# Local and global attention with a gated feed-forward layer: loads paced in the planner, exponentials of 21 tiles turned by transfers, and every engine's order laid anew

## The chip, the cores and the metric

The kernel runs on one core of a Trainium2 chip. A core has five instruction streams: TensorE (PE, matrix products, with its weight loads shown as PEld), VectorE (DVE), ScalarE (ACT), GpSimd (POOL) and SyncE (SP). SP does no arithmetic here; it issues transfers, as GpSimd does too. The transfers themselves run on 16 DMA engines that all streams share. The metric is device time in microseconds (us), lower is better; a profile is one more execution, whose span is counted from its first to its last instruction.

## What is computed

Eight batches of eight heads attend over 32 global and 512 local positions; a local query sees the global keys and the local keys at most 32 positions away. All 544 output positions of a batch then go through a feed-forward layer. Cut to what matters:

```python
s_g   = scale * q_g @ concat(k_g, k_l).T
out_g = softmax(s_g) @ concat(v_g, v_l)
s_ll  = where(abs(i - j) <= 32, scale * q_l @ k_l.T, -1e9)
out_l = softmax(concat(scale * q_l @ k_g.T, s_ll)) @ concat(v_g, v_l)
x = concat(out_g, out_l).reshape(8 * 544, 512)       # heads side by side
h = x @ w_in                                          # 512 -> 2048
out = (h * clip(h + 3, 0, 6) / 6) @ w_out             # 2048 -> 512
```

## The kernel before

**Units of work.** Local attention works on 32 tiles, one for each batch b and each 128 queries j. A tile passes through: S, the scores of its eight heads (line 810, 32 short matmuls); per head a mask-and-maximum on DVE (822) and an exponential on ACT (826); E, the turning of the exponentials; A, their product with the values (853); a normalisation on DVE (865, 867); X, the turning of the result into `xt`. E and X are done either on PE with a copy out of PSUM (839 and 874, copies at 372 on ACT and 374 on DVE), or by a transposing transfer that SP issues (354); the strings `ETURN` and `XTURN` say which for each tile. Each batch also has one global tile (Sg line 912, Ag line 956). Queries and keys of a batch are turned on PE in one of two forms, 64 small matmuls (691) or 32 larger ones (728); `WIDE` lists the batches of the second form. The values are loaded to `vn`, and A needs them in overlapping strips `vs`; a strip is either copied ("moved", 634 on ACT, 636 on DVE and POOL) or transferred by SP (608 and the transfer below it); `MOVED` and `MOVERS` say which, and by which engines.

**Feed-forward.** M1 (994) makes one of 16 column chunks of the hidden layer with four matmuls, ACT and DVE gate it (1000, 1004), M2 (1020) multiplies by `w_out`, ACT or DVE copies the result out (1031, 1033), SP stores it. Batch 0 does M1 in halves of 256 tokens, the others with 512.

**Loads.** Nearly all loads from memory convert to fp16 and are issued by GpSimd (344). GpSimd also moves strips, in one order with the loads.

**Order.** No order is written by hand. The program first runs a planner (`Plan`): a list of operations with costs, dependencies and ranks is played through in simulated time, and the order in which the operations start there becomes the instruction order of each engine. Loads queue in `queues["POOL"]`; `able` says whether an operation may start; `fetch` models that PE's instructions come in blocks of 256 that are fetched while it runs, and adds a delay when a block would come late. PE's choice is made by `pick` with a due value `key` for each operation, built from `LEAD`, `KEYS`, `STEP`; while PE has nothing to do at the beginning, `warm` fills it with dummy matmuls (1138). `ORDER` is the order of the first loads and `OFF` shifts the ranks of DVE's and ACT's work in the first two batches. Nothing of the planner's time exists on the chip: there each engine runs its fixed order and waits for what the operands need, and GpSimd's load also waits until the eighth load before it has landed.

Of the kernel before, what the change touches and what calls it, by code (L numbers as in the profile page):

```python
# [33 lines left out]
class Plan:  # L34
# [10 lines left out]
    def add(self, engine, cost, emit, deps=(), rank=(0,), lat=None, mode="full", take=(), give=(), what=""):  # L45
        if isinstance(cost, tuple) and engine == "PE":
            cost, count = cost
        else:
            count = 0
        op = Op(engine, cost, emit, deps, self.LAT[engine[0] if isinstance(engine, tuple) else engine]  # L50
                if lat is None else lat, rank, mode, take, give, what)
        op.count = 2 * count
        self.ops.append(op)
        return op

    BLOCK, AHEAD, FETCH = 256, 60, (3900.0, 5500.0, 7500.0)

    def fetch(self, n, cost, keep=True):

        late, used, come = 0.0, self.used, {}  # L60
        for i in range(n):
            at = self.now + cost * i / n + late
            used += 1
            if used % self.BLOCK == 0:
                b = used // self.BLOCK
                wait = max(come.get(b, 0.0), self.come.get(b, 0.0)) - at
                if wait > 0:
                    late += wait
                    at += wait
            if (used + self.AHEAD) % self.BLOCK == 0:  # L70
                come[(used + self.AHEAD) // self.BLOCK + 1] = at + self.FETCH[2 if self.queues["POOL"] else 1 if self.queues["SP"] else 0]
        if keep:
            self.used = used
            self.come.update(come)
            self.stall += late
        return late

    def run(self, pick):
# [32 lines left out]
        def drain():  # L111
# [15 lines left out]
                        count += 1  # L127
            moved_at[0] = self.now

        def look():  # L130
            nonlocal count
            live = share()
            moved_at[1] += 1
            if live:
                heapq.heappush(events, (self.now + min(q[0][1] / part for q, part in live) + 1e-6, count, moved_at[1]))
                count += 1

        def able(op, e):
            if e == "SP" and sum(x[0].cost[3] for x in queues["SP"][1:]) > 300:
                return False  # L140
            if op.units and op.units > self.ring:
                return False
# [42 lines left out]
        while len(order) < len(self.ops):  # L185
            moved = True
            while moved:
                moved = False
                for e in ("PE", "ACT", "DVE", "POOL", "SP"):
# [11 lines left out]
                    op = pick(self, can) if e == "PE" else min(can, key=lambda o: (o.rank, o.at))  # L201
# [10 lines left out]
            while events and events[0][0] <= t + 1e-9:  # L212
                op = heapq.heappop(events)[2]
# [19 lines left out]
def kernel(  # L233
# [12 lines left out]
    nc = tc.nc  # L246
# [4 lines left out]
    S = Sg + Sl  # L251
# [74 lines left out]
    plan = Plan()  # L326
    add = plan.add
# [12 lines left out]
    DMA_LAT = 1500.0  # L340
    LOAD_LAT = 1800.0

    def load(dst, src, rows, run, deps, rank, what):
        op = add("POOL", dma(rows, run), lambda: nc.gpsimd.dma_start(out=dst, in_=src), deps, rank, LOAD_LAT,  # L344
                 what=what)
        op.units = 1
        return op

# [45 lines left out]
    HELD = ("S3", "A2", "A2")  # L394

    def hold(what):
        return what and (s_op if what[0] == "S" else av_op)[0][int(what[1])]


    OFF = ((-2.5, -9, -2.0, -2, -3.0, 5.5, -9, 6.5, -0.5, -0.5), (0, 1, -5.5, -1, 0, 1.0, 9, 1, -4.0, 1.5))  # L400
    WORKS = ("Tc", "Vc", "max", "exp", "Ec", "move", "norm", "Xc", "glob", "gate")

    def line(b, j, what, *more):
# [27 lines left out]
    wz = add("DVE", 200.0, lambda: nc.vector.memset(xs[0], 0.0), rank=(-2,), what="zero x")  # L431
# [54 lines left out]
    GLOBAL = {0: (1, 2), 1: (1, 3)}  # L486
# [619 lines left out]
    ffn_global()  # L1106


    PACE, LEAD, SLACK, STEP, WAIT, LATE = 1, 3, 30, 4, 1000, 100
    EARLY = 60000  # L1110
    KEYS = (42, 10, 32, -14, 41)
    state = {"since": 0, "fed": False}
    PIECES = 2 * NDFF

    def key(op):
        if op.key is None:
            r, w = op.rank, op.what
            if w == "Places":
                op.key = -1e9
            elif r[0] == B:  # L1120

                op.key = B * PIECES + (r[2] if w == "M1" else NDFF + 4 * r[1] + r[2])
            elif w == "M1":
                op.key = r[0] * PIECES + 2.0 * (r[2] + r[1] * 0.5)
            elif w[0] == "M":
                op.key = (r[0] + 1) * PIECES + 2.0 * (4 * r[1] + r[2]) + 1
            elif w[0] in "VTG":
                op.key = (r[0] - 1) * PIECES - LEAD - STEP * (2 - 0.25 * min(r[2] * 2, 4)) + KEYS[0]
            else:
                op.key = (r[0] - 1) * PIECES - LEAD + STEP * (r[2] + 2 * (r[1] - 1)) + KEYS[1 + (w[0] == "A") + 2 * (w[-1] == "g")]  # L1130
        return op.key
# [20 lines left out]

    def pick(plan, can):
        if not can:
            cold = not state["fed"] and wz.done is not None and wz.done <= plan.now and plan.free["m"]
# [12 lines left out]
        if m is not None and plan.now >= EARLY:  # L1168

            due = [o for o in tiled if key(o) <= key(m)]  # L1170
            tiled = [o for o in tiled if key(o) <= key(m) + SLACK]
            if plan.pe_mode == "full" and (not due or len({o.mode for o in tiled}) < 2 and
                                           all(plan.now - o.ready < WAIT for o in due)):
                tiled = []
        if m is not None:
            tiled = [o for o in tiled if plan.fetch(o.count, o.cost, False) < LATE]
        if tiled and (m is None or plan.pe_mode != "full" or state["since"] >= PACE or plan.now < EARLY):
            same = [o for o in tiled if o.mode == plan.pe_mode]
            order = {"64x128": 0, "32x128": 0, "64x64": 1, "128x64": 1, "64x32": 2, "128x32": 3}
            if plan.pe_mode == "full":  # L1180
                state["since"] = 0
            return min(same or tiled, key=lambda o: (order[o.mode], key(o), o.at))
        if m is not None:
            state["since"] += 1
        return m
# [6 lines left out]
    order = plan.run(pick)  # L1192
# [36 lines left out]
```

## Time and profile before

| | us |
|---|---|
| three timed runs: median (lowest, highest) | 333.29 (332.99, 336.12) |
| profiled execution: its own time | 334.7 |
| its span | 332.9 |
| PE busy in the span | 319.3 |
| DVE busy | 249.3 |
| ACT busy | 229.6 |
| POOL busy | 192.8 |

The time of the profiled execution is 1.8 us more than its span, and 1.4 us more than the median of the timed runs. The PE clock is full all the way. A table of stretches gives for each stretch the busy time of an engine in us; a busy PE may still be slower than its best, because a matmul's end is modelled.

### The profile page before, as it was taken

How to read it: one execution, taken by the hardware profiler on the slowest of the kernel's cores; microseconds unless marked ns; L12 is line 12 of the kernel's file. 1: busy time of each engine (PE TensorE's matmuls, PEld its weight loads, DVE VectorE, ACT ScalarE, POOL GpSimd, SP SyncE). 2: the span in 40 equal slices, each digit the busy share in tenths (PEclk: the TensorE clock that was granted, in tenths of full speed). 3: DMA queues.
4: the chain of work that ended last, by engine and by line, in shares of the span. 5: the costliest groups of instructions: out<-in, count | busy, mean ns of one | idle time of the engine just before them, and what ended most of it. 6: DMA issues, size and time to landing. Idle time of an engine off the chain costs nothing.

```text
span 332.9 us, 12451 instructions
## 1 busy us (share of the span) xinstructions
PE 319.3 (96%) x4966; PEld 165.7 (50%) x4966; DVE 249.3 (75%) x1001; ACT 229.6 (69%) x554; POOL 192.8 (58%) x303
## 2 busy tenths in 40 slices
PE   8999878999999998999999999999899999999996
PEld 3447556555545543454445444444344444446644
DVE  5799999889999798678797778768897682456400
ACT  3699899878988679479897658647477651465502
POOL 8599687999159989959997899904850000000000
PEclk9999999999999999999999999999999999999999
DMA  8999999988459979699799998369947715100013
GB/s 132 210 206 202 192 210 120 198 158 124 89 54 176 187 121 147 117 137 153 176 105 113 168 198 138 83 148 81 127 59 157 175 35 102 69 28 7 32 56 103
DMA packets 107082, 42.35 MB, mean 127 GB/s; under 512 B 85136, under 2 KB 102800, under 8 KB 107024
## 3 DMA queue, kind: packets, MB, share of 16 engines
q0 software_dynamic: 53136, 17.47, 53.6%
q1 hardware_dynamic: 53888, 24.08, 38.2%
q8 instruction: 39, 0.64, 0.8%
q14 instruction: 19, 0.16, 0.2%
HBM read 35.13 MB, written 8.91 MB: 132 GB/s over the span
## 4 chain that ended last, share of the span: by engine, by line
PE 73%; DVE 15%; DMA 5%; ACT 3%; issue 3%; POOL 0%; DVEq 0%; ACTq 0%; POOLq 0%
PE m L1020 28%; PE m L994 24%; PE t L1020 4%; PE t L994 4%; DVE vs L636 4%; DVE gl L1004 3%; PE s L810 3%; PE a L853 3%; DVE sm L822 3%; DMA gT<-gn 2%; DMA vn<-in_v_l_dram 2%; PE t L839 2%; DVE x L867 2%; DMA kn<-in_k_l_dram 2%; ACT t L1000 1%
## 5 line engine op out<-in xcount | busy, mean ns | idle before, releaser
L636 POOL COPY vs<-vn 32x528 f16<-32x528 f16 (+1 forms) x190 | 118.7, 625 | 17.4 <-DMA vn<-in_v_l_dram 2.6
L1020 PE MATMUL m<-wout,gl 128*128 128x512 f16 (+1 forms) x480 | 113.5, 376 | 0.3 <-DVE gl L1004 0.3
L994 PE MATMUL m<-xt,win 128*128 128x512 f16 (+1 forms) x508 | 107.3, 352 | 5.9 <-DVE gl L1004 3.9
L1004 DVE SCALAR_TENSOR_TENSOR gl<-t,m 128x512 f16<-128x512 f32 (+1 forms) x140 | 81.8, 598 | 29.5 <-ACT t L1000 28.1
L826 ACT ACTIVATE ex<-sm,mx 128x128 f16<-128x128 f32 x256 | 83.0, 398 | 18.7 <-DVE mx L822 17.8
L1000 ACT ACTIVATE t<-m 128x512 f32<-128x512 f32 (+1 forms) x140 | 73.2, 536 | 28.3 <-PE m L994 27.1
L994 PEld LDWEIGHTS <-win 128*128 128x128 f16 x640 | 60.4, 98 | 62.9 <-issue 9.6
L1020 PEld LDWEIGHTS <-gl 128*128 128x128 f16 x560 | 51.7, 98 | 53.8 <-issue 1.0
L822 DVE CUSTOM_DVE_ANT_0 sm<-s,mask 128x128 f32<-128x128 f32 x256 | 59.1, 286 | 12.9 <-PE s L810 11.6
L1031 ACT COPY ot<-m 128x512 f32<-128x512 f32 (+1 forms) x19 | 10.9, 572 | 23.4 <-PE m L1020 23.3
L867 DVE TENSOR_TENSOR x<-a,rec 128x256 f16<-128x256 f32 x64 | 24.2, 418 | 0.1
L344 POOL DMA_DIRECT2D vn<-in_v_l_dram x24 | 21.2, 895 | 1.2 <-DMA kn<-in_k_l_dram 0.7
L822 DVE DVE_READ_ACCUMULATOR2_ANT mx<- 128x1 f32 x256 | 21.3, 83 | 0.0
L344 POOL DMA_DIRECT2D vn<-in_v_g_dram x7 | 4.1, 587 | 28.9 <-PE a L956 28.6
L1020 PE MATMUL t<-wout,gl 128*128 128x512 f16 (+1 forms) x80 | 18.9, 358 | 0.4 <-DVE gl L1004 0.4
L994 PE MATMUL t<-xt,win 128*128 128x512 f16 x68 | 17.5, 379 | 1.2 <-DVE gl L1004 1.2
L636 DVE COPY vs<-vn 64x528 f16<-64x528 f16 (+1 forms) x36 | 16.2, 451 | 2.7 <-DMA vn<-in_v_l_dram 1.9
L372 ACT COPY et<-t 128x1024 f16<-128x1024 f16 (+1 forms) x15 | 14.6, 971 | 5.2 <-PE t L839 5.2
L1004 DVE SCALAR_TENSOR_TENSOR gl<-t,t 128x512 f16<-128x512 f32 (+1 forms) x20 | 12.9, 647 | 6.7 <-ACT t L1000 6.6
L1000 ACT ACTIVATE t<-t 128x512 f32<-128x512 f32 (+1 forms) x20 | 11.3, 564 | 8.6 <-PE t L994 8.4
L344 POOL DMA_DIRECT2D kn<-in_k_l_dram x22 | 14.5, 683 | 0.8 <-POOLq L1213 0.8
L853 PE MATMUL a<-vs,et 128*32 128x65 f16 x1024 | 14.3, 195 | 0.4 <-DVE x L867 0.2
(109 smaller groups left out, 304.6 us busy)
## 6 DMA issues: line engine op xcount, KB each, us to landing
out_dram<-ot SPq DMA_DIRECT2D x31, 256.0 KB, 3.2
vs<-vn SPq DMA_DIRECT2D x14, 264.0 KB, 5.0
kn<-in_k_l_dram POOLq DMA_DIRECT2D x14, 256.0 KB, 10.4
qn<-in_q_l_dram POOLq DMA_DIRECT2D x14, 256.0 KB, 7.7
vn<-in_v_l_dram POOLq DMA_DIRECT2D x24, 128.0 KB, 6.4
wout<-in_moe_w_out_dram POOLq DMA_DIRECT2D x8, 256.0 KB, 8.1
win<-in_moe_w_in_dram POOLq DMA_DIRECT2D x4, 512.0 KB, 11.6
gl<-in_v_l_dram POOLq DMA_DIRECT2D x8, 128.0 KB, 9.1
```

The source lines that it names most:

```text
L344: op = add("POOL", dma(rows, run), lambda: nc.gpsimd.dma_start(out=dst, in_=src), deps, rank, LOAD_LAT, what=what)
L372: nc.scalar.copy(out=dst(), in_=src())
L636: (nc.vector if o.on == "DVE" else nc.gpsimd).tensor_copy(out=dst, in_=src)
L822: nc.vector.tensor_tensor_reduce(out=sm[i3][h], in0=pss[e][:, p * P:(p + 1) * P], in1=m, scale=-scale, scalar=3.0e38, op0=ALU.add, op1=ALU ...
L826: nc.scalar.activation(out=ex[ie][:, h, :], in_=sm[i3][h], func=EXP, scale=-1.0, bias=mx[i3][h])
L853: nc.tensor.matmul(out=psa[h // 4][q, c0:c0 + D + 1], lhsT=et[k][:, h * P + u * Sg:h * P + (u + 1) * Sg], rhs=vs[r][:, j * UJ + u, h, 0:D ...
L867: nc.vector.tensor_tensor(out=xs[ix][:, 4 * c * D:4 * (c + 1) * D].rearrange("q (h d) -> q h d", d=D), in0=acc[c][:, :, 0:D], in1=rr[c].to ...
L994: nc.tensor.matmul(out=ps[:, 0:n], lhsT=w_in[:, m, c * P:(c + 1) * P], rhs=x(m), start=(m == 0), stop=(m == NP - 1))
L1000: nc.scalar.activation(out=t1[st["t"]][:, 0:n], in_=pm[st["m"]][:, 0:n], func=RELU, bias=0.5, scale=1.0 / 6.0)
L1004: nc.vector.scalar_tensor_tensor(out=g, in0=t1[st["t"]][:, 0:n], scalar=1.0, in1=pm[st["m"]][:, 0:n], op0=ALU.min, op1=ALU.mult)
L1020: nc.tensor.matmul(out=pm[st["m"]][:, 0:n], lhsT=g[c][:, t0:t0 + P], rhs=w_out[:, c, cols], start=(c == 0), stop=(c == NDFF - 1))
L1031: nc.scalar.copy(out=ot[st["o"]][:, 0:n], in_=pm[st["m"]][:, 0:n])
```

## The change

The planner is changed, and the settings that it works from.

```diff
+    PACED, DEPTH = 30000.0, 2
-    BLOCK, AHEAD, FETCH = 256, 60, (3900.0, 5500.0, 7500.0)
+    BLOCK, AHEAD, FETCH, WAITS = 256, 60, (3900.0, 5500.0), 4200.0
...
-                come[...] = at + self.FETCH[2 if self.queues["POOL"] else 1 if self.queues["SP"] else 0]
+                self.drain()
+                behind = min(self.WAITS, sum(x[1] for x in self.queues["POOL"]))
+                come[...] = at + max(self.FETCH[0] + behind, self.FETCH[1] if self.queues["SP"] else 0.0)
...
-            if op.units and op.units > self.ring:
+            if op.units and (op.units > self.ring or self.now > self.PACED and len(queues["POOL"]) >= self.DEPTH):
                 return False
...
+    MARGIN = 1500.0
-                 LOAD_LAT, what=what)
+                 LOAD_LAT + (MARGIN if what[0] in "vqkg" and int(what[2]) > 2 else 0.0), what=what)
...
-    ORDER = "k0 q0 id v0 o4 v1 bd K o3 w3 Q w1 V w0 w2 o5 G o7 o2 o0 o6 o1".split()
+    ORDER = "q0 k0 id v0 w0 o4 Q bd v1 o6 o1 w1 K V G w3 o7 o3 o0 w2 o5 o2".split()
-    EM, XM = set(), {(b, j) for b in range(2) for j in range(4)}
+    EM, XM = {(b, j) for b in range(2) for j in range(4)}, set()
-    ETURN = "00000000 00000011 00101011 11111111"
-    XTURN = "00000000 11111111 10110111 11111111"
+    ETURN = "00000000 11101110 10111111 11111111"
+    XTURN = "00000000 11001001 00010110 11011111"
-    MOVERS = {b: ("POOL",) if b < 7 else ("POOL", "DVE") for b in range(2, 8)}
-    WIDE = (0, 1)
+    MOVERS = {b: ("POOL",) if b < 6 else ("POOL", "ACT") for b in range(2, 8)}
+    WIDE = (0, 1, 2)
-    MOVED = {(b, j) for b in range(8) for j in range(4)}
+    MOVED = {(b, j) for b in range(8) for j in range(4) if b != 1 or j < 1}
...
-        gate = [s_op[b - 2][0]] if b >= 2 else []
+        gate = [av_op[b - 2][0]] if b >= 2 else []
...
-    PACE, LEAD, SLACK, STEP, WAIT, LATE = 1, 3, 30, 4, 1000, 100
-    KEYS = (42, 10, 32, -14, 41)
+    PACE, LEAD, SLACK, STEP, WAIT, LATE = 1, 40, 2, 4, 4000, 400
+    KEYS = (30, 30, -20, 40, 27)
-    PAIR, LAG = 99, 2
+    PAIR, LAG = 16, 3
```

`OFF`, `HELD` and `GLOBAL` get other values too, and three further settings are added with values that change nothing. In words: after 30 us of planned time a load is planned only while fewer than two others are in its queue; a block of PE's instructions is planned to come later the more load work is queued; exponentials of 21 tiles instead of 14 and results of 14 instead of 22 are turned by transfers; the strips of batch 1 are transferred by SP except for its first tile; batches 6 and 7 may move strips on ACT, and batch 7 no longer on DVE; the queries and keys of batch 2 are turned in the wider form. Since the orders come out of the planner, nearly every engine's order differs.

More of the change, by code (lines that the diff above doesn't have):

```diff
@@ L70, in fetch @@
             if (used + self.AHEAD) % self.BLOCK == 0:
-                come[(used + self.AHEAD) // self.BLOCK + 1] = at + self.FETCH[2 if self.queues["POOL"] else 1 if self.queues["SP"] else 0]
+                self.drain()
+                behind = min(self.WAITS, sum(x[1] for x in self.queues["POOL"]))
+                come[(used + self.AHEAD) // self.BLOCK + 1] = at + max(self.FETCH[0] + behind, self.FETCH[1] if self.queues["SP"] else 0.0)
         if keep:
@@ L128, in drain @@
             moved_at[0] = self.now
+        self.drain = drain
         def look():
@@ L341 @@
     LOAD_LAT = 1800.0
+    MARGIN = 1500.0
     def load(dst, src, rows, run, deps, rank, what):
-        op = add("POOL", dma(rows, run), lambda: nc.gpsimd.dma_start(out=dst, in_=src), deps, rank, LOAD_LAT,
-                 what=what)
+        op = add("POOL", dma(rows, run), lambda: nc.gpsimd.dma_start(out=dst, in_=src), deps, rank,
+                 LOAD_LAT + (MARGIN if what[0] in "vqkg" and int(what[2]) > 2 else 0.0), what=what)
         op.units = 1
@@ L382 @@
     TURNS0 = ((0, (0, 1), "a"), (1, (0, 1), "s"))
-    EM, XM = set(), {(b, j) for b in range(2) for j in range(4)}
+    EM, XM = {(b, j) for b in range(2) for j in range(4)}, set()
     G0 = 1
-    ETURN = "00000000 00000011 00101011 11111111"
-    XTURN = "00000000 11111111 10110111 11111111"
+    ETURN = "00000000 11101110 10111111 11111111"
+    XTURN = "00000000 11001001 00010110 11011111"
     QT = (7,)
-    MOVERS = {b: ("POOL",) if b < 7 else ("POOL", "DVE") for b in range(2, 8)}
-    WIDE = (0, 1)
-    HELD = ("S3", "A2", "A2")
+    MOVERS = {b: ("POOL",) if b < 6 else ("POOL", "ACT") for b in range(2, 8)}
+    WIDE = (0, 1, 2)
+    HELD = ("S3", "A3", "A3")
     def hold(what):
         return what and (s_op if what[0] == "S" else av_op)[0][int(what[1])]
-    OFF = ((-2.5, -9, -2.0, -2, -3.0, 5.5, -9, 6.5, -0.5, -0.5), (0, 1, -5.5, -1, 0, 1.0, 9, 1, -4.0, 1.5))
+    OFF = ((-1, -6.0, -9, -4.0, -3.5, 0, -2, 0, 8.0, 5.0), (-0.5, 1.0, 1.5, 8.5, -3.0, 0, -3.5, 2.5, -5.0, 5.5))
     WORKS = ("Tc", "Vc", "max", "exp", "Ec", "move", "norm", "Xc", "glob", "gate")
@@ L485 @@
     TURNS = ((0, (0, 1), "s"), (1, (0, 1), "a"))
-    GLOBAL = {0: (1, 2), 1: (1, 3)}
+    GLOBAL = {0: (1, 0)}
     vperm = [[] for _ in range(B)]
@@ L1106 @@
     ffn_global()
-    PACE, LEAD, SLACK, STEP, WAIT, LATE = 1, 3, 30, 4, 1000, 100
+    PACE, LEAD, SLACK, STEP, WAIT, LATE = 1, 40, 2, 4, 4000, 400
     EARLY = 60000
-    KEYS = (42, 10, 32, -14, 41)
+    KEYS = (30, 30, -20, 40, 27)
+    REST = 0
+    KEYED, GLAST = 0, 0
     state = {"since": 0, "fed": False}
@@ L1154, in pick @@
         if not can:
-            cold = not state["fed"] and wz.done is not None and wz.done <= plan.now and plan.free["m"]
+            cold = not state["fed"] and wz.done is not None and wz.done <= plan.now and plan.free["m"] and (plan.now < WARM or plan.now - plan.busy["PE"] >= REST)
             return warm() if cold else None
@@ L1181, in pick @@
                 state["since"] = 0
-            return min(same or tiled, key=lambda o: (order[o.mode], key(o), o.at))
+            return min(same or tiled, key=lambda o: (0 if plan.now < KEYED else order[o.mode] + GLAST * (o.what[0] == "S" and o.what[-1] == "g"),
+                                                     key(o), o.at))
         if m is not None:
```

## The prediction

> **What bounds the kernel now.** First the page: engine shares, then PE's slices.
>
> ```profile
> PE 319.3 (96%) x4966; PEld 165.7 (50%) x4966; DVE 249.3 (75%) x1001; ACT 229.6 (69%) x554; POOL 192.8 (58%) x303
> ...
> PE   8999878999999998999999999999899999999996
> ```
>
> PE is the bound, with 13.6 us idle in a span of 332.9. Where that idle time lies, I asked of stretches (length, then PE, PEld, DVE, ACT, POOL; the last three numbers are the clock, the DMA share and GB/s):
>
> ```profile
> 30.00:57.00 27.00, 22.37 (x426) 16.57 (x411) 25.63 (x86) 25.52 (x65) 19.99 (x32) 1.00 1.27 179
> 57.00:130.00 73.00, 72.92 (x1484) 38.07 (x1485) 66.31 (x301) 60.47 (x153) 57.43 (x90) 1.00 1.03 141
> 130.00:134.00 4.00, 2.29 (x72) 1.16 (x69) 2.71 (x5) 2.66 (x5) 3.65 (x7) 1.00 1.65 145
> 134.00:233.00 99.00, 98.81 (x1676) 48.08 (x1675) 76.70 (x340) 71.96 (x176) 75.88 (x116) 1.00 1.20 133
> 233.00:245.00 12.00, 9.86 (x135) 4.47 (x134) 10.71 (x29) 6.37 (x16) 10.09 (x16) 1.00 0.91 100
> ```
>
> The reader sees three holes: 4.6 us in 30 to 57, where DVE and ACT are both busy 25.6 and 25.5 of 27; 1.7 us at 130 to 134; 2.1 us at 233 to 245. Between them PE loses 0.3 us. PE's waits name the causes:
>
> ```profile
> PE m L994 <- DVE gl L1004: 3.9, 8, 1.1
> PE m L994 <- issue: 1.7, 1, 1.7
> PE t L994 <- DVE gl L1004: 1.2, 1, 1.2
> ```
>
> The first line lies wholly within 30 to 57: M1 of batch 0 waits for its gates. The second is the hole at 131, waiting for nothing the profile shows: a fetch of PE's instructions of 16 KB began at 130.3 and took 1.6 us. The third, at 235.7, begins the hole in which DVE moves strips of batch 7 in front of gates, since their values were issued only at 228.2 and landed at 233.9.
>
> **The change, part by part, against 334.7 us (the profiled execution's own time).**
>
> *PE's work.* I counted the groups of matmuls in both built orders and priced them by starts in the trace: 0.216 us for a matmul of 512 columns, 0.109 for 256, 0.45 for an E on PE, 0.23 for an X, 0.65 for a batch's q or k turned in 64 matmuls and 1.04 in 32, 0.1 at each return from short tiles to full ones. Seven fewer E: -3.2. Eight more X: +1.9. Batch 2 turned wide, 2 x 0.39: +0.8. Two more dummy matmuls: +0.4. Returns: +0.3. Sum **+0.2** (314.6 to 314.8 us in all). What follows the last attention tile is the same sequence, so the tail stays. Below, a *position* is such a priced sum up to a place in the order, and the *lag* is how far the chip ran behind it: 4.2 us at position 18, 5.0 at the first M1, 11.0 at time 57, 13 at the end.
>
> *The beginning.* Before its first M1 PE does the same work in both orders, with 65 dummies in place of 63. Loads come in another order: batch 0's second half of values stands behind 1 `w_in` piece, 1 `w_out` piece and batch 1's queries. Pieces of `w_in` landed about 2.5 us apart, of `w_out` 1.25, a half of q 1.3; so it lands some 6 us later than the 14.5 of now, at 20 to 21, and PE asks for it at about 23 (position 18.8 plus a lag of 4.2). Covered by 2 us.
>
> In 30 to 57 DVE and ACT decide. Batch 1's strips leave them: up to the 32nd gate (batch 0's last) DVE has 11 fewer strip copies (24 to 13), ACT 4 fewer (14 to 10), POOL 8 fewer (22 to 14). With all other copies, priced by each group's mean (0.45 us a strip copy on DVE, 0.63 on ACT, 0.69 and 0.60 a turned q or k, 1.01 an `et` copy on ACT), DVE's list up to that gate falls from 65.5 to 62.2 us and ACT's from 60.1 to 57.2. Means overlap; busy time over the sum of means is 0.82 for DVE and 0.85 for ACT: **-2.7 and -2.5 us**. I take -2.5. Bounds: -4.6, all idle time of that stretch, and 0, if something else ends last there.
>
> What replaces them: SP issues eight more transfers of strips behind two that issue at 39.5 and 40.1 now. At 0.6 us each the last is issued near 46; strips took 8.2 to 9.4 us in the busy stretches; landed by 55. The second tile of batch 1 reads them at position 50.3, which with a lag of 11.0 - 2.5 is 58.8. Covered by 4 us; if the values come later, every us beyond that is lost. Behind these SP has a transfer of global operands and batch 2's strips, which nobody reads for 10 us.
>
> *The hole at 131.* Loads and the fetch shared the DMA engines there (share 1.65 in the table's stretch). In the new order GpSimd puts one to three strip copies (0.62 us each) between loads that stood in fours and eights. I take **-1.9**, this stall with its refill; bound 0.
>
> *The hole at 233.* Batch 7's values may be loaded once Ag of batch 5 is done. Its priced position moves from 213.9 to 204.4, the strips' reader only from 255.8 to 252.7, and DVE moves no strips of batch 7 (12 before). **-2.1**; bound 0.
>
> *New waits.* A turned exponential is now used sooner. From S to A there are, in priced PE work, 21 us or more for every transferred E now, but 12.9, 12.3 (batch 2), 10.9, 13.7 (3), 14.1 (4) and 12.9 us (7) for the tightest later. From S to its landing the trace shows 9.8 us (S at 178.15; issue at 183.3, 4.6 to landing) to 18.3, median 12.6 over nine tiles whose ACT was not late; the two longest were issued only 13 and 15 us after S, the next is 16.1. At 12.6 the tiles (2,1) and (3,0) lack 0.3 and 1.7 us: 2.0. Batch 3's last X has 5.0 us between A and M1 of batch 4; an X landed 3.8 us after A when nothing else moved and 10.7 to 12.0 under loads. The new order has no load there, so I take 5.7: 0.7. Together **+2.7**, the lower end being 0 and the upper, at 16.1 and 10.7 where a load lies near, (3.8 + 5.2 + 2.0 + 5.7) = 16.7. A lower end below 0 is excluded, for these waits do not exist now.
>
> ACT's 16 and 13 strip copies of batches 6 and 7 (29 x 0.63 = 18 us) fall in 190 to 250 where ACT is 56 to 70% busy; ranks put gates first. I cost them at nothing; if ACT is late there, E of batch 7 is next. GpSimd loses 25 copies (15.6 us), and its loads queue behind fewer.
>
> Sum: 0.2 - 2.5 - 1.9 - 2.1 + 2.7 = **-3.6**, 331.1 for a profiled execution, which lies 1.4 above the median: **329.7 us**.
>
> **A rule weighed.** With eight loads under way an X took 9.1 and 9.7 us to land, with none 2.4:
>
> ```profile
> L354 SPq DMA_TRANSPOSE xt<-x x2: 1221/1846/2471, 138.1 to 141.7; - x2
> ...
> DMA to landing us min/median/max: 9.1/9.4/9.7
> ```
>
> The Trainium skill (DMA: Bandwidth & Descriptors, section "SWDGE vs HWDGE vs iDMA") says that GpSimd's transfers and SP's sit in different internal queues of a DMA engine, which takes turns between them. By that rule the share of a transpose is the same behind two loads as behind eight, and pacing would buy nothing. The trace neither confirms nor refutes it: it shows 6.0 us at 108.1, with two loads still to land, between the two.
>
> **Rivals.**
>
> *Late transposes (slower).* The tight tiles meet loads all the same, and any number of loads delays a transpose as eight do. GpSimd gets no new wait on the chip, only another order; its loads are still issued as fast as it comes to them, so this is also the case in which the change does not do what it says. For it: three of nine E landed after 16 us or more, and A now stands where the planner believes it ready, with no slack. Against: that planner's order let PE lose 0.3 us in 172 us. It decides from a mean S-to-landing of about 14 us; at 16.1 and 10.7, 0.2 - 2.5 - 1.9 - 2.1 + 16.7 = +10.4, 343.7; with half of the tiles so, +2.1, about 335.5, and with the fetch stall kept 337.
>
> *No gain at the beginning (about the same).* M1 of batch 0 is then held by something else: values of batch 1 late, or gates that wait for PE and not for DVE. For it: PE's own order between 30 and 57 carries the same pieces, and DMA is already full there (share 1.27), with 8 transfers more. Against: DVE and ACT at 95%. 334.7 + 0.2 - 4.0 + 2.7 = 333.6, median 332.2; with the hole at 131 kept, 334.
>
> **How the numbers follow.** A measurement of this kernel tells about 1% from no change, 3.3 us. The forecast has 0.47, the case of about the same 0.34, late transposes 0.19. All of the forecast case lies near the 1% line (330.0); its upper edge, to 331, is balanced by the case of no gain at the beginning with smaller new waits, so faster 0.47, same 0.35, slower 0.18. Range: if new waits cost nothing and the beginning gains 4.6, 334.7 + 0.2 - 4.6 - 4.0 - 1.4 = 324.9, which is unlikely altogether; 326 to 336.5 leaves the full late transposes out and holds the rest.
>
> **What would show it.** Right: PE's idle time in the beginning below 3 us and batch 0's M2 starting 2.5 us before 59.1; no wait of PE on "issue" over 1 us; no hole of PE before A of batch 7; waits of A on `et` transfers of 1 to 3 us in sum. Wrong: PE waiting for DMA `et<-ex` or `xt<-x` for more than 6 us, the stretch up to 57 with as much idle time as now, or a wait on `vs` transfers in batch 1.

## The result, and the profile after

| | before | after |
|---|---|---|
| median of 20 runs each, us | 333.41 (331.48 to 336.65) | 330.40 (329.44 to 334.86) |
| ratio after/before, 95% interval | | 0.9908 [0.9886, 0.9930] |
| profiled execution, us | 334.7 | 331.21 |
| its span, us | 332.9 | 329.4 |

The kernel is 0.9% faster, 3.0 us in the medians and 3.5 us between the two profiled executions; forecast were 3.6. In some executions the granted clock falls to half for 3.4 us or a multiple of it, and medians called *undisturbed* below are of the executions without such a fall (mean clock of 0.998 and more), which flatters kernels with long waits of PE, since the falls come with these (last section).

The page of after, first the engines, then PE's slices:

```profile
PE 318.2 (97%) x4880; PEld 164.4 (50%) x4880; DVE 239.3 (73%) x987; ACT 237.2 (72%) x571; POOL 174.9 (53%) x278
...
PE   8999968999899999999999999999999999999995
```

VectorE has lost 10 us of work, GpSimd 18, ScalarE gained 8. PE's thin slices are now two from 41 to 58 us and one at about 86. The stretches of before, asked of after (length, then PE, PEld, DVE, ACT, POOL busy; clock, DMA share, GB/s):

```profile
30.00:57.00 27.00, 23.14 (x450) 17.42 (x449) 24.58 (x102) 25.05 (x70) 12.71 (x20) 1.00 1.23 202
57.00:130.00 73.00, 71.58 (x1359) 36.48 (x1359) 62.30 (x270) 54.63 (x137) 57.11 (x90) 1.00 1.34 145
130.00:134.00 4.00, 4.00 (x63) 2.21 (x62) 4.00 (x12) 3.10 (x6) 3.72 (x7) 1.00 1.19 222
134.00:233.00 99.00, 98.54 (x1698) 47.72 (x1697) 81.57 (x346) 84.74 (x201) 77.72 (x121) 1.00 1.14 141
233.00:245.00 12.00, 11.33 (x121) 5.12 (x119) 3.43 (x9) 5.15 (x9) 0.21 (x1) 1.00 0.67 120
```

The hole at 131 is gone (4.00 of 4.00), the one at 233 has shrunk from 2.1 us to 0.7, and a new one of 1.4 lies in 57 to 130. PE's waits in after:

```profile
PE m L1003 <- DVE gl L1013: 3.1, 4, 1.5
PE a L862 <- DMA et<-ex: 1.2, 1, 1.2
PE m L1003 <- DMA win<-in_moe_w_in_dram: 1.1, 1, 1.1
```

No wait on "issue" is left in this execution. Two waits are new: A of tile (2,1) waits 1.2 us for its turned exponentials (at 90 us), and M1 of batch 0 waits 1.1 us for the last piece of `w_in` (at 49).

Because a busy PE may be slower than its best, I measure places by the lag of the prediction: real start minus priced position in PE's order.

| place | lag before | lag after | after minus before |
|---|---|---|---|
| end of the beginning (time 57) | 11.1 | 9.2 | -1.9 |
| ahead of the old hole at 131 | 10.8 | 10.0 | -0.8 |
| behind it | 12.8 | 9.7 | -3.1 |
| ahead of the old hole at 233 | 12.5 | 10.8 | -1.7 |
| last M2 | 14.9 | 11.1 | -3.8 |

With the 0.2 us that the priced work grew, the last M2 starts 3.6 us earlier (326.4 to 322.8). Between 150 and 200 us after slips by 1.1 us against its prices without PE being idle for it (the table of stretches has 0.3 us more idle time in 134 to 233); that is a price of mine a little too low there, and I did not follow it further.

### The profile page after: what moved, and what is told of

Read it like the earlier page. It is cut to its first block, busy times and chain, and to the rows that moved or that the text cites. A ratio compares the mean times of both kernels' runs of the same rounds, so it can differ in the third digit from the quotient of the medians.

```text
span 329.4 us, 12254 instructions
## 1 busy us (share of the span) xinstructions
PE 318.2 (97%) x4880; PEld 164.4 (50%) x4880; DVE 239.3 (73%) x987; ACT 237.2 (72%) x571; POOL 174.9 (53%) x278
## 4 chain that ended last, share of the span: by engine, by line
PE 75%; ACT 9%; DMA 7%; DVE 5%; issue 2%; POOL 1%; ACTq 0%
PE m L1029 30%; PE m L1003 23%; PE t L1029 4%; ACT ex L835 4%; PE t L1003 3%; PE m L1149 3%; DMA win<-in_moe_w_in_dram 3%; PE a L862 3%; DMA et<-ex 3%; PE s L819 2%; ACT t L1009 2%; DVE gl L1013 2%; DMA vn<-in_v_l_dram 1%; ACT vs L643 1%; PE t L883 1%
## 5 line engine op out<-in xcount | busy, mean ns | idle before, releaser
L1003 PE MATMUL m<-xt,win 128*128 128x512 f16 (+1 forms) x536 | 114.3, 354 | 4.2 <-DVE gl L1013 3.1
L1029 PE MATMUL m<-wout,gl 128*128 128x512 f16 (+1 forms) x496 | 117.7, 376 | 0.1
L645 POOL COPY vs<-vn 64x528 f16<-64x528 f16 (+1 forms) x165 | 102.5, 621 | 22.0 <-ACT vn L381 5.7
L1013 DVE SCALAR_TENSOR_TENSOR gl<-t,m 128x512 f16<-128x512 f32 (+1 forms) x147 | 86.3, 601 | 24.2 <-ACT t L1009 23.8
L643 ACT COPY vs<-vn 32x528 f16<-32x528 f16 (+1 forms) x39 | 24.5, 628 | 0.8
L1149 PE MATMUL m<-ident 128*128 128x512 f16 x57 | 15.6, 392 | 0.0
L862 PEld LDWEIGHTS <-et 128*32 128x32 f16 x1024 | 10.2, 96 | 10.9 <-issue 7.3
L1013 DVE SCALAR_TENSOR_TENSOR gl<-t,t 128x512 f16<-128x512 f32 (+1 forms) x13 | 8.1, 624 | 9.7 <-ACT t L1009 9.7
L1029 PE MATMUL t<-wout,gl 128*128 128x512 f16 (+1 forms) x64 | 14.8, 353 | 0.0
L874 DVE RECIPROCAL rec<-a 128x4 f32<-128x4 f32 x64 | 8.5, 167 | 7.9 <-PE a L862 7.9
```

The lines of the kernel that those rows point to most:

```text
L643: nc.scalar.copy(out=dst, in_=src)
L645: (nc.vector if o.on == "DVE" else nc.gpsimd).tensor_copy(out=dst, in_=src)
L862: nc.tensor.matmul(out=psa[h // 4][q, c0:c0 + D + 1], lhsT=et[k][:, h * P + u * Sg:h * P + (u + 1) * Sg], rhs=vs[r][:, j * UJ + u, h, 0:D ...
L1003: nc.tensor.matmul(out=ps[:, 0:n], lhsT=w_in[:, m, c * P:(c + 1) * P], rhs=x(m), start=(m == 0), stop=(m == NP - 1))
L1013: nc.vector.scalar_tensor_tensor(out=g, in0=t1[st["t"]][:, 0:n], scalar=1.0, in1=pm[st["m"]][:, 0:n], op0=ALU.min, op1=ALU.mult)
L1029: nc.tensor.matmul(out=pm[st["m"]][:, 0:n], lhsT=g[c][:, t0:t0 + P], rhs=w_out[:, c, cols], start=(c == 0), stop=(c == NDFF - 1))
```

## The experiments

All ratios are to before. Wherever a kernel is said to keep its orders, the planner's result was taken as it stands, and only the list behind it was edited, so that PE's order stays the same.

### The beginning: batch 1's strips

Edit of after: the eight transfers of batch 1's strips are replaced by the copies they stand for, dealt to VectorE (9), ScalarE (7) and GpSimd (7), in the transfers' places.

```diff
+    turn = iter("DPADPADPADPADPADPADPADD")
+    def copied(o):
+        for dst, src in o.pieces:
+            e = next(turn)
+            ...tensor_copy on DVE or POOL, copy on ACT...
+    for o in order:
+        if hasattr(o, "pieces"):
+            o.emit = lambda o=o: copied(o)
```

> The changed kernel with its order kept on every engine, except that batch 1's strips (all but the first tile's) are copied on DVE (9), ACT (7) and POOL (7) where SP issued the 8 transfers. Theory (the beginning is held by DVE and ACT, and the strips' leaving them is most of its gain): the lag at 57 us grows from 9.2 by about 2 us, time 332.4 (ratio to the kernel before about 0.997). Rival (the beginning gains by the order of loads and gates, the strips do not matter): within 0.5 us of 330.4 (ratio 0.990 to 0.992).

Measured: ratio to before 1.0106 [1.0068, 1.0145]; undisturbed median 336.26 us of 5 runs, against 333.24 of before on the same chip. The first 57 us of this kernel, a stretch and two of PE's waits:

```profile
30.00:57.00 27.00, 20.21 (x356) 14.70 (x357) 24.16 (x88) 25.71 (x64) 18.59 (x29) 1.00 1.24 169
```

```profile
PE m L1004 <- DVE gl L1014: 6.5, 9, 2.2
PE m L849 <- DVE gl L1014: 1.5, 2, 1.1
```

PE is idle 6.8 us of the 27 in place of 3.9, and all but 0.3 of it waits for gates. The lag at priced position 48 is 13.7 in place of 9.2, and the last M2 has a lag of 16.0 in place of 11.1: what is lost at the beginning is never given back. So the copies of batch 1's strips ahead of batch 0's gates are enough to undo the gain at the beginning. That they cost 4.5 us here and not the 2 that were expected is no measure of the change itself: in before the planner had laid the copies out between the gates, and here they stand where transfers stood.

The converse, in before: batch 1's strips but its first tile's sent by eight transfers, the orders kept.

```diff
+    sent = [o for o in order if o.what in ("move1.1", "move1.2", "move1.3")]
+    order = [o for o in order if o not in sent]
+    at = 1 + max(i for i, o in enumerate(order) if o.what[:4] == "Vc1." or o.what == "strip1.g")
+    ...eight times nc.sync.dma_start(out=dst, in_=src), put in at this place...
```

> The kernel before with its order kept, except that batch 1's strips (all but the first tile's) are sent by 8 transfers of SP, behind the last copy that makes its values, and no longer copied. Theory: the idle time of PE in 30 to 57 us falls from 4.6 by 1.8 to 2.5 us, time 331.2 (ratio 0.994). Rival (strips do not matter, or the transfers land late for the second tile of batch 1): ratio 0.998 to 1.003.

Measured: ratio 1.0116 [1.0059, 1.0173], slower than before, where both theory and rival had it faster or the same. The profile says why; its stretch and its waits:

```profile
30.00:57.00 27.00, 22.83 (x437) 17.20 (x437) 23.75 (x80) 24.27 (x62) 14.10 (x22) 1.00 1.24 210
```

```profile
PE m L995 <- issue: 2.9, 1, 2.9
PE m L995 <- DVE gl L1005: 2.3, 4, 1.2
PE s L811 <- DVE mx L823: 1.7, 1, 1.7
PE a L692 <- DMA kn<-in_k_l_dram: 1.3, 1, 1.3
```

The wait for gates falls from 3.9 us to 2.3 and the lag where batch 0's M1 ends from 11.1 to 9.25: the relief is there, 1.9 us, as large as in after's profile. (The idle time of the stretch falls by 0.5 us only, because 1.1 us of the wait for keys lies in it.) But batch 2's keys now come late (1.3 us, at 57), a tile's scores wait for VectorE's maxima (1.7 us, at 69, with a fall of the clock right behind), and the fetch stall of 131 grows from 1.7 us to 2.9. So here the strips alone bring the gain of the beginning, and an order that was not laid for it loses it again.

### The last piece of w_in

Here stood a wait that the prediction does not have. The chain of waits of after, around 38 to 49 us (start, length, what):

```profile
37.91 0.58 ACT vn L381
...
38.55 0.63 POOL vs L645
...
39.23 0.63 POOL vs L645
39.86 9.51 DMA win<-in_moe_w_in_dram
```

GpSimd issues the last piece of `w_in` only at 39.9, since two strip copies of batch 1 stand ahead of it and those waited for ScalarE:

```profile
POOL vs L645 <- ACT vn L381: 5.7, 1, 5.7
```

Edit of after: that load ahead of the two copies, nothing else moved.

```diff
+    late = [o for o in order if o.what == "win"][-1]
+    order.remove(late)
+    order.insert(next(i for i, o in enumerate(order) if o.what == "move1.0" and o.on == "POOL"), late)
```

> The changed kernel with one step of GpSimd's order changed: the last piece of w_in is issued ahead of the two strip copies of batch 1 that wait 5.7 us for ACT. Theory (PE's wait of 1.1 us for that piece is a loss of its own): the wait goes, time 329.3 (ratio 0.9875). Rival (gates are next and take the same time): 330.2 or more (0.990), with PE's wait on gates up by 1 us.

Measured: the load is issued at 32.6, the wait for it is gone, and the lag at position 48 is 8.5 in place of 9.2, a gain of 0.75. At 74 us nothing of it is left: there an X on PE waits 0.6 us for VectorE's normalised result, which it does not in after. As a time it is inconclusive: the one undisturbed run took 329.74, the five others 335.7 to 339.5, and no ratio was formed. And in its profile the tile (2,1), read below, waits longer:

```profile
PE a L862 <- DMA et<-ex: 3.9, 1, 3.9
```

GpSimd now comes sooner to batch 4's queries and issues them at 80.7 and 81.3, ahead of that tile's transpose at 81.9. In after the transpose was issued at 81.7 and the queries behind it, from 82.2 on. One load moved ahead brought two others in front of a transfer that PE was about to need.

### The hole at 131

Edit of before: two value loads and two strip transfers of batch 4 moved behind the place of the stall, the rest kept.

```diff
+    for what, n in (("vn4.2", 5), ("vn4.3", 7)):
+        o = next(o for o in order if o.what == what)
+        order.remove(o)
+        order.insert(order.index(moves[n]), o)
+    ...and the two "strip4.g" behind the next transfer of an X of batch 3...
```

> The kernel before, with the two value loads and two strip transfers of batch 4 that were under way about 130 us moved later, so that no load is under way when PE's block of instructions is fetched there. Theory of the prediction (loads shared the DMA engines with the fetch): PE's wait on issue at 131 falls from 1.7 to below 0.5 us and the lag rises there by 0.3 or less in place of 1.9; ratio 0.994 to 0.996 if nothing else is late for it. Rival (the wait comes from where the block's edge lies in PE's order, whatever is loaded): the wait on issue stays at 1.5 to 2 us, ratio 0.999 to 1.003.

Measured: ratio 1.0025 [0.9985, 1.0064], no change. The profile has the two halves of that, a stretch and a wait:

```profile
130.00:134.00 4.00, 4.00 (x122) 2.04 (x123) 3.89 (x8) 3.96 (x10) 2.91 (x5) 1.00 1.37 185
```

```profile
PE m L994 <- DMA xt<-x: 3.4, 2, 2.9
```

At the same position in the same order the lag rises by 0.1 us, where it rises by 2.0 in before, by 2.2 and 3.2 in the two other kernels made from before (the strips of batch 7 on ScalarE, and batch 1's strips sent), which kept these loads. So the place of the block's edge alone does not make the stall, and the transfers bunched there are its likely cause. It is one profile of each kernel, and such stalls also come and go by themselves at other places (last section). The fetch itself took 1.2 us here and 1.6 in before, so most of the 2 us lies ahead of it, in getting started. What was moved away from the fetch then stood around the last transposed result of batch 3, which came 2.9 us late, more than was gained.

### The hole at 233

Edit of before: batch 7's 12 strip copies of VectorE put on ScalarE, in their places.

```diff
+    for o in order:
+        if o.what[:6] == "move7." and o.on == "DVE":
+            o.on = "ACT"
```

> The kernel before, with batch 7's 12 strip copies of VectorE on ScalarE instead, in the same places. Theory of the prediction (DVE's copies ahead of gates make the hole of 2.1 us at 233 to 245): most of the waits of PE for gl at 235 to 244 go, lag there +1 or less in place of 2.7; 1.3 to 2 us faster, ratio 0.994 to 0.996. Rival (the values of batch 7 landed too late at 233.9, whoever copies the strips): the hole stays at 2 us or more, ratio 0.998 or above; ACT is then the one that PE waits for.

Measured: ratio 1.003 [0.9982, 1.0079]; undisturbed median 333.81 of 7 runs, before 333.51. Of its profile, the stretch of the hole and what is left of waits for gates and products in it:

```profile
233.00:245.00 12.00, 11.85 (x146) 5.43 (x145) 7.41 (x25) 9.75 (x18) 10.35 (x15) 1.00 1.49 145
```

```profile
PE a L853 <- DVE x L867: 0.8, 1, 0.8
PE m L1020 <- DVE gl L1004: 0.2, 1, 0.2
```

The place lies 3 to 4 us later here, so the lag is the fairer measure: over the hole it rises by 1.3 in place of 2.7. VectorE's copies ahead of the gates were half of the hole, where the prediction had all of it. In the profile this relief of 1.4 us stays to the last M2. The profiled time is longer all the same, for 4 us were lost at 113 to 116, where the order is still that of before: 2.3 us of a wait on "issue" and a fall of the clock behind it. The timed runs show no gain, and their interval holds one of 0.2%, 0.6 us, at most; why they show less than the profile's 1.4 us stays open.

### Tile (2,1), and loads behind each other

A of tile (2,1) is the only local tile in after that waits for its turned exponentials. The chain has it as

```profile
80.20 1.46 ACT ex L835 x5
81.68 9.02 DMA et<-ex
```

The transfer is issued at 81.7 as soon as the exponentials are there; four loads of batch 4's q and k are issued at 82.2 to 85.2. Two kernels ask what these loads do.

Edit of after, first: each load after 50 us is followed at once by up to seven more that could go, so that loads stand behind each other as they did in before.

```diff
+    for i, o in enumerate(order):
+        ...
+        if o.units and o.start > 50000:
+            more = [x for x in order[i + 1:] if x.units and id(x) not in early][:7]
+            for x in more:
+                if all(place[id(d)] < i or id(d) in early for d in x.deps):
+                    out_order.append(x); early.add(id(x))
+                else:
+                    break
```

> The changed kernel with every engine's order kept except GpSimd's, where after 50 us of planned time a load that follows others with strip copies between is put directly behind them, as long as everything that it depends on stands ahead. Theory (spacing loads keeps transposes and fetches early): landing of turned exponentials goes up by 1 to 3 us, PE waits on them or on issue for 1.5 to 4 us more, time 332 to 334 (ratio 0.995 to 1.003). Rival (the spacing does nothing on the chip, its rule shapes the order alone): within 0.6 us of 330.4 (0.989 to 0.993).

Measured: ratio 1.0104 [1.0055, 1.0154]; the profiled run, undisturbed, took 334.98 us against 331.21 of after's. Most of the difference lies in one line, which is 1.2 in after:

```profile
PE a L862 <- DMA et<-ex: 3.8, 1, 3.8
```

Two of the four loads, the queries, are now issued ahead of the transpose (81.8 and 82.4 against 82.5), the lag rises there by 3.8 in place of 1.2, the last M2 has 14.9 in place of 11.1, and no other new wait exceeds 0.7 us. It is the picture of the kernel with `w_in` ahead: two loads ahead of the transpose and more right behind it, and a wait of 3.8 and 3.9 us. One transposed tile among bunched loads costs as much as the whole change gains.

Second: the four loads held until that tile has landed, by a copy of one column of it on GpSimd ahead of them.

```diff
+    def seen(src):
+        return Op("POOL", 0, lambda: nc.gpsimd.tensor_copy(out=mark[0:Sg, :], in_=src()), ...)
+    late = [o for o in order[:at] if o.what == "qn4"]
+    order = [o for o in order[:at] if o not in late] + [seen(lambda: et[1][0:Sg, 0:1])] + late + order[at:]
```

> The kernel after, with the q and k loads of batch 4 held on GpSimd until the turned exponentials of tile (2,1) have landed (a copy of one column of that tile stands ahead of them). Theory (the one late transpose was issued at 81.7 and four loads came right behind it, 82.2 to 85.2, which stretched it to 8.8 us): it lands in 4 to 5 us, PE's wait of 1.2 us for et<-ex at tile (2,1) is gone and the span is 1.2 us shorter than after's 329.4, about 328.2; ratio to before 0.987. Rival (the transpose was late because of what was under way before it, or the exponentials were late): the wait stays at 1 us or more, span 329 to 330. Second rival (the loads of batch 4 are then late themselves): a wait of PE for in_q or in_k near 100 us, span above 330.

> The kernel after, with both the last piece of w_in loaded ahead of the two strip copies of batch 1 that held it up on GpSimd, and batch 4's q and k loads held until tile (2,1) has been turned. Theory: the 1.1 us of waiting for w_in at the beginning gives 0.75 (as the run with this piece alone showed by position 48) and the transposed tile 1.2; span about 327.5, ratio to before 0.984 to 0.986. Rival (what is gained at the beginning is lost again by a tile that comes due sooner): lag at the beginning 0.75 lower than after's, a new wait of PE for a transpose of 1 us or more behind it, and the same span as with the held loads alone.

Measured: 0.9962 [0.9927, 0.9997] alone and 0.9933 [0.9895, 0.9971] with `w_in` ahead as well; undisturbed medians 331.76 and 331.31, before 333.51 on that chip. The theory holds for this wait: the one for `et<-ex` is gone in both, and no wait for batch 4's loads stands in its place, so the second rival falls. The only wait for a load in the second of them is

```profile
PE a L738 <- DMA qn<-in_q_l_dram: 1.2, 1, 1.2
```

(1.1 us in the first). I read it as batch 4's queries, held too long. That was wrong: the wait ends at 7.6 us (7.9 in the first), and L738 turns in the wide form, which only batches 0 to 2 use. It is batch 0's queries at the very start. The second kernel gains 1.3 us on after at tile (2,1), but its span of 328.5 is only 0.9 below after's and not 1.9: of the 0.7 us that `w_in` ahead had brought at 50 us, 0.15 were left at 74.

The next run was built on that misreading: only the keys are held, together with `w_in` ahead, and after was run again beside it.

```diff
-    late = [o for o in order[:at] if o.what == "qn4"]
+    late = [o for o in order[:at] if o.what == "kn4"]
```

> The kernel after with the last piece of w_in loaded ahead of the two strip copies, and only batch 4's k loads (not its q loads) held until tile (2,1) is turned. Theory (four loads behind the transpose stretched it, and the q loads held in the earlier runs came 1.2 us too late themselves): neither et<-ex nor in_q is waited for; the lag after that tile is 8.6 to 9.0 where the run with all four held has 8.97 and after 10.35, and with no wait for q the kernel is 1.2 us faster than that one: span about 327.3, ratio to after 0.993 to 0.995. Rival (DMA is simply full from 64 to 92 us, so that whatever is put first makes the other late): one of et<-ex, in_q or in_k is waited for by 1 us again, and the span is 328.5 or more.

> The kernel after once more, unchanged, on the same chip as the two runs beside it, so that they can be compared with it. Ratio to before 0.989 to 0.993 as before. The profile again shows a wait of PE for et<-ex at tile (2,1) of 1 to 1.5 us and one for the last piece of w_in of about 1.1 us.

Measured on one chip: after 0.9904 [0.9862, 0.9945], undisturbed median 330.74 of 8 runs; with both edits 0.9926 [0.9894, 0.9958], 331.00 of 10. Both profiles have a span of 328.4. Two waits of the edited kernel:

```profile
PE t L884 <- DVE x L877: 0.5, 1, 0.5
...
PE a L738 <- DMA qn<-in_q_l_dram: 0.4, 1, 0.4
```

and of after in this second execution:

```profile
PE m L1003 <- DVE gl L1013: 3.1, 5, 1.5
...
PE s L700 <- issue: 0.9, 1, 0.9
PE a L737 <- DMA qn<-in_q_l_dram: 0.8, 1, 0.8
```

The reader sees that the two waits I set out to remove, for `w_in` and for `et<-ex`, are not in this execution of the unchanged kernel at all. The 0.8 us are batch 0's queries again, at 7 us; the 0.9 us on "issue" lie at 81. The last piece of `w_in` lands at 48.29, and PE takes it up at 48.35. After stands at an edge in these two places, and the waits come and go between executions.

What the wait for `w_in` costs is not lasting either. At 50 us the second execution of after and the three kernels with `w_in` ahead are 0.7 to 0.8 us ahead of after's first profile; at 81 none is more than 0.2 us ahead. The three lost it, one of them not quite, at 73 us, two in a wait of an X on PE for VectorE (the 0.5 us above is one); the second execution of after lost it at 81, by the wait on "issue". The wait at tile (2,1) does last: without it, the second execution of after and the kernel with only the keys held both end 1.0 us ahead. So the expected span of 327.3 was missed by 1.1 us, no load is waited for in its place, and removing the two waits gains nothing that the times show. Nothing run here beats after.

### What pacing is

Edit of after: each load after 50 us waits on the chip until the second load before it has landed.

```diff
+    for o in order:
+        if o.units:
+            if o.start > 50000:
+                paced.append(seen(lambda d=loaded[-2].dst: d[0:Sg, 0:1, 0]))
+            loaded.append(o)
+        paced.append(o)
```

> The kernel after, with each of GpSimd's loads after 50 us really held until the second load before it has landed (a copy of one column of that load's tile stands ahead of it), which is what the title of the change says and what the chip does not do in after (more than two were under way for 99 us). Theory (pacing is an order, and the gain does not come from fewer loads under way at once): et<-ex and xt<-x land faster, median 3 us or less, but 68 loads in pairs of 4 us cannot be done in time, so q, k or values of later batches are late: PE waits for in_q, in_k or vs by 3 us or more and the time is 1 to 5% above after. Rival (what makes the change is that fewer loads are under way): no wait for loads over 1 us, the wait for et<-ex at tile (2,1) gone, ratio to after 0.995.

Measured: 374.79 us, ratio 1.1213 [1.1143, 1.1282]. Three of PE's waits, 37 us together:

```profile
PE m L1004 <- DVE gl L1014: 19.0, 9, 7.4
PE s L701 <- DMA qn<-in_q_l_dram: 10.9, 2, 9.0
PE a L701 <- DMA kn<-in_k_l_dram: 6.9, 2, 4.4
```

Queries and keys are late, and the gates too. The wait stands in GpSimd's one order, so it holds back GpSimd's strip copies together with the loads; the two are not separated here. Both kernels' transposes of exponentials, after first, then this one:

```profile
DMA to landing us min/median/max: 2.6/4.3/7.8
```

```profile
DMA to landing us min/median/max: 2.6/4.1/9.8
```

They land hardly sooner in the median, against the theory, and the loss is far beyond the 1 to 5% that I expected. The rival is out as well, since queries and keys are waited for. That the title's rule is not what after's chip does is plain: there more than two loads were under way for 99 us between 55 and 250, and for 87 in before.

Last, after with the planner's limit lifted (99 in place of 2), and everything laid anew by it.

```diff
-    PACED, DEPTH = 30000.0, 2
+    PACED, DEPTH = 30000.0, 99
```

> The kernel after with the planner's limit on loads under way lifted (99 in place of 2), everything else of the change kept; the planner then lays all orders anew by itself. Theory (the gain comes from batch 1's strips by transfer, which leaves VectorE and ScalarE free before batch 0's gates; pacing only keeps loads from standing behind each other near the turned exponentials): the beginning gains as in after, lag at batch 0's last M1 8.5 to 9.5 in place of 11.1, and one or more waits for et<-ex or xt<-x of 1 to 4 us in sum come in later; ratio to before 0.992 to 1.003. Rival (pacing carries the gain): the beginning loses too, ratio 1.005 or more. Second rival (pacing is worth nothing): ratio 0.989 to 0.992 as after and no wait for et<-ex or xt<-x above 0.5 us.

Measured: 343.12 us, ratio 1.0277 [1.0224, 1.0331]. The profiled run of 342.9 has two falls of the clock, at 7 and 171 us, each behind a wait of PE (1.6 and 3.7 us); the fastest run took 339.78, still slower than before. None of the three theories holds as stated. The beginning keeps its gain: from batch 0's first M1 to its first M2 this kernel takes 26.5 us, as the second execution of after does, where after's first profile has 27.3 and before 28.9. Behind that the lag rises by some 13, one fall of the clock among it, where after's rises by about 2. PE's longest waits, of which 2.5 of the 3.3 us for gates lie in the beginning:

```profile
PE a L862 <- DMA et<-ex: 3.7, 1, 3.7
PE m L1003 <- DVE gl L1013: 3.3, 6, 1.5
PE m L1029 <- DVE gl L1013: 1.6, 2, 1.0
...
PE a L700 <- issue: 1.3, 1, 1.3
```

A wait on "issue" is back, and three turned exponentials took 10.8, 12.0 and 15.0 us to land, with five to eight loads under way. The other settings were kept as they are for the paced order, so this is the price of leaving the limit out of this planner's work, not of loads alone.

## Why the prediction was right, and where not

The total was right, -3.5 between the two profiles against -3.6. That it is right to 0.1 is luck: the second execution of after is another 1.0 us shorter, and the terms, right in kind, miss by up to 1.5 us in the first profile and in part cancel.

- **The beginning, -2.5.** The mechanism is shown by the two strip experiments, from both sides, and by the kernel without the limit, which keeps the gain. The size is 1.9 in after's profile and 2.65 in its second execution (lag 8.47 at 57). What was missed is a queue: I followed the loads of batch 0's values and counted pieces of `w_in`, but not that its last piece stands in GpSimd's order behind two strip copies that wait 5.7 us for ScalarE. PE waits 1.1 us for it in one execution and not at all in the other, and what that costs is made up again by 81 us. The marks I gave were too bold: PE's idle time in 30 to 57 is 3.9 and 3.1 us, not below 3, and batch 0's M2 starts at 57.7 and 56.9, 1.4 and 2.2 us before 59.1.
- **The hole at 131, -1.9.** Right in size (2.0 by the lag), and the cause is supported: with the loads moved away, the same fetch at the same place costs 0.1, in one profile. The sign I gave, no wait on "issue" over 1 us, holds in both profiles of after. It is not safe: with the same order up to that place, the first kernel with batch 4's loads held had one of 2.2 us that ended at 84.
- **The hole at 233, -2.1.** The idle time there fell by 1.5, from 2.1 to 0.7; one wait for a gate is left. By moving the copies alone 1.4 of a rise of 2.7 went. The step that failed is that all of the hole was put down to VectorE's copies and late values; 0.7 us of it had another cause, which I did not separate.
- **New waits, +2.7.** Mis-sized: 1.2 in one execution, none of this kind in the other. I summed two tiles at a median of 12.6 us from S to landing, taken from before, and the last X of batch 3; the tile (3,0), which was to bring 1.7, and the X did not wait at all. In after the transfers of the six tight tiles are issued 4 to 7 us behind S, and the four of them whose landing is recorded landed 7 to 11 us behind it. The other tile, (2,1), is late by what is issued around it: 0, 1.2, 3.8 or 3.9 us in four executions of one PE order. It is not late with the loads held behind it, nor with the two loads of the queries ahead of it and the keys held.
- **Work of PE, +0.2.** Right by the prices; where the profile could show it, it is lost in the 1.1 us of lag that I cannot account for.

**The rivals.** "No gain at the beginning" fell by the table of lags. "Late transposes" did not come about in after, but its mechanism exists: bunched loads bring 3.8 us of it at one tile, and landings of 10 to 15 us come back where the planner lays its order without the limit. Its second half, that the change does not do what it says because loads are paced in the planner only, is true of the chip and yet decides nothing, since the order alone keeps loads from the tight tiles.

**The rule of the Trainium skill** (DMA: Bandwidth & Descriptors, section "SWDGE vs HWDGE vs iDMA"). Over 14 traces of this study, a turned exponential landed in 3.6 us (median of 118) with no load of GpSimd under way at its issue, 4.1 with one (33), 4.6 with two (24), 7.2 with three (13), 7.2 with four (21) and 6.6 with five (9); where a landing was not recorded, the next load's was taken. The rule, by which GpSimd's transfers and SP's have queues of their own that a DMA engine serves in turn, would give the same from the first load on. The traces do not agree from one to three loads, where the time rises by three quarters; from three to five they do. SP's own transfers, of which more are under way where loads are many, explain little of it: with no load under way the median stays at 3.5 to 4.0 us with none to four of them. The count is of loads at the issue. Loads issued right behind a transpose stretch it too, as tile (2,1) shows; the first X of the prediction's example, too, had two loads under way at its issue and six more within 3.6 us. Why holding loads to two gained the transposes almost nothing in the median fits this: most were issued with two or fewer under way in after too.

## What to carry to other kernels

Ask of each load that is moved not only what is under way beside it but what stands ahead of it on the engine that issues it: a copy that waits for another engine holds up every load behind it. A limit on loads under way belongs into the planner that lays the order, where it moves loads away from transfers that are about to be needed; as a wait in GpSimd's order it cost 12% here. And before a wait of 1 us in one profile is worked on, ask when it happens, and not only which line waits; a second profile of the same kernel then shows whether it is there at all.

## What the runs showed of the hardware

- A fetch of PE's instructions, 16 KB for a block of 256, took 0.9 to 1.7 us in all of the profiles of before and after, mostly beside other transfers; at one place of before's order PE stood still for it, for 2.0, 2.2 and 3.2 us of lag in three kernels, and for 0.1 once loads and strip transfers had been moved away. The DMA share of those 4 us was 1.65, 2.21 and 1.42 against 1.17: the share does not order them.
- The waits on "issue" go with such fetches: in 14 profiles PE has twelve of them over 0.3 us, and each ends 1.25 to 2.0 us after a fetch of 16 KB has ended. They come and go where the order is the same: 0, 0.9 and 2.2 us at 81 to 84 (after twice, and batch 4's loads held), 0 and 2.3 us at 113 to 116 (before, and batch 7's strips on ScalarE).
- Ahead of the last instructions the 14 profiles have twelve falls of the clock to half, of 3.4 us or two or three times that. Each lies in a wait of PE of 1.6 us or more, or begins at most 1.3 us behind its end; seven waits of 1.7 to 3.8 us outside of falls brought none. In the four profiles where it can be read apart, a fall of 3.4 us put PE back by 1.3 to 1.9 us beside the wait. So a long wait of PE can cost this much more than its own length.
- The landing of a transpose rises in a step between two and three loads under way (4.6 to 7.2 us), and hardly from there to five.
